# A segment-recurrent attention kernel with a channel MLP: all engines' orders in a block written down whole, each scaled probability write as two operations

## The chip, the cores and the metric

The kernel runs on one core of a Trainium2 chip. The metric is the device time of one launch in microseconds (us). A core has five engines with queues of their own: TensorE (PE in the profile; its weight loads are PEld), VectorE (DVE), ScalarE (ACT), GpSimd (POOL) and SyncE (SP), which issues DMAs.

## What is computed

A layer norm of x (2048 x 512) goes through attention that runs over 64 segments of 32 rows. Each segment sees 8 memory rows ahead of its own, and the attention's first 8 output rows are the memory of the next segment, so segments follow one another. Behind it stands a channel MLP on all rows.

```python
for s in range(n_seg):                       # 64 segments
    xs = x[:, s*32:(s+1)*32, :]
    h = concatenate([mem, xs], axis=1)       # 8 + 32 rows
    q, k, v = h @ Wq, h @ Wk, h @ Wv         # 32 heads of 128
    p = softmax(where(mask, q @ k.T * scale, -1e9))
    o = einsum('bhte,hed->btd', p @ v, Wo)
    mem = o[:, :8, :]
    outs.append(o[:, 8:, :])
h = x + concatenate(outs, axis=1)
y = layernorm(layernorm(h))
h2 = h + gelu(y @ w1 + b1) @ w2 + b2
```

## The kernel before

**How the work is staged.** All weights of the attention lie in SBUF. A block is 4 segments (128 rows of x); s mod 4 is called a segment's *kind* here. A segment has these parts, each a list of recorded operations: `Q0`, `Q1`, `K0`, `K1`, `V0`, `V1` (a projection's two halves, four units each; a unit is four matmuls of 512 columns in tiles of 128 rows x 32 columns, side by side in the array), `SC0` and `SC1` (scores of the memory's queries for half of the heads), `PV0` and `PV1` (their probabilities times values), `PVA` (the same for the 24 other rows, of the segment before), `WO` (eight units of sixteen instructions: output projection), `SA` (scores of the other rows), and `F0`, `F1`, eight units of work that isn't on the segment's own path: in kinds 0, 1, 2 the K, Q, V projections of the next block's last rows, in kind 3 the output projection `wo_B` of the block before. Blocks 0 and 15 have none or few of them. PV0, PV1 and PVA are in tiles of 64 x 128, all other parts named here in tiles of 128 x 32.

**The path through a segment.** Q0 to K1 are copied out of PSUM by ScalarE (`kq0` to `kq3`), transposed by VectorE (`QT`, `KA`), and the memory's queries are laid into `ZC` (`ZCm0`, `ZCm1`, GpSimd). SC0 goes to `sc_softmax`: a maximum on VectorE (`nmc`), two exponentials with their sums on ScalarE (`EC`), then on VectorE for each of the two column sets a reciprocal (`ra`, `rsc`) and a scaled probability write (`PCa`, `PC`), and a transpose (`PTC0`), for which PV0 waits. SC1, PTC1 and PV1 go the same way. PV0's and PV1's results are copied to `OT` (`OTm0`, `OTm1`), WO reads them, VectorE transposes WO's result (`TT`) and adds its halves into `hT` (`hTm`): the memory rows, for which the next segment's Q0 waits. SA's softmax runs beside this path (`nma`, `SA`, `sma`, `rsa`, `PA`, `PTA`) and ends in four GpSimd copies (`BD`), which PVA reads a segment later.

**What sets the order.** Every operation is recorded with what it reads and writes. TensorE's order is written by hand in `ORDERS`: for each kind a list of (part, first unit, end). For the other engines `Sched.schedule` places operations in time: `PLAN` gives an operation's time from its segment's start by kind of operation and of segment, for priority alone; `HOME` names the engine of some that can run on two; else the scheduler takes the free place and the engine that end earliest. Operations that aren't on the path are held behind others by `after=`: the layer norm of a coming block (`ln1`) behind the memory rows, `PA` behind the memory rows, `ZCb` (`qb_fill`) behind KA0, the residual rows (`opA`) and the end of a block's statistics (`nat`) behind PTC1, GpSimd's fold of `wo_B`'s result (`fold`) behind the probability writes. `wire` turns orders into semaphore waits. `align` puts spare weight loads into TensorE's stream so that each segment starts at a given place (`PHASE`) of a block of 256 fetched instructions.

The write whose form is changed, in `sc_softmax` (`even` is 128 x 2, ones in one column for even groups of 32 rows and in the other for odd ones):

```python
S.op("dve", lambda e, sl=sl, xc=xc: e.scalar_tensor_tensor(PC[:, r, :, :, sl], xc, rsc[:, r, sl:sl + 1], ev, ALU.mult, ALU.mult),
     reads=[ek, rk, "even"], writes=[pk], dur=0.305)
```

Of the kernel before, what the change touches and what calls it, by code (L numbers as in the profile page):

```python
# [40 lines left out]
ORDER = ORDERS[0]  # L41
BANK = dict(K0=7, K1=6, Q0=6, Q1=5, V0=7, V1=5, F0=4, F1=6, FB=4, SA=5, WO=7, SC0=3, SC1=2)
PLAN = {"kq2": (1.72,) * 4,
        "QT0": (2.37,) * 4,
        "ZCm0": (2.85,) * 4,
        "kq0": (2.23,) * 4,
        "KA0": (2.87,) * 4,
        "SP0": (-5.14, -4.54, -4.55, -4.02),
        "nmc0": (3.86,) * 4,
        "Ea0": (4.18,) * 4,  # L50
        "EC0": (4.59,) * 4,
        "ra0": (4.66,) * 4,
        "PCa0": (4.86,) * 4,
        "rsc0": (5.1,) * 4,
        "PC0": (5.4,) * 4,
# [1 line left out]
        "VS0": (4.88,) * 4,
        "kq3": (2.79,) * 4,
        "QT1": (3.48,) * 4,
        "ZCm1": (3.97,) * 4,  # L60
        "kq1": (3.65,) * 4,
        "KA1": (4.29,) * 4,
        "SP1": (-1.16, -1.01, -1.18, -1.31),
        "nmc1": (5.19,) * 4,
        "Ea1": (5.51,) * 4,
        "EC1": (5.92,) * 4,
        "ra1": (5.98,) * 4,
        "PCa1": (6.1,) * 4,
        "rsc1": (6.35,) * 4,
        "PC1": (6.55,) * 4,  # L70
        "PTC1": (7.13,) * 4,
        "VS1": (5.61, 5.61, 6.51, 6.21),
        "VSl1": (6.65, 6.5, 6.56, 6.5),
        "OTm0": (6.05, 6.05, 6.05, 6.2),
        "OTm1": (6.85, 7.84, 7.9, 6.64),
        "OTB": (9.67, 11.69, 9.8, 10.06),
        "SAp": (7.58, 6.98, 8.18, 7.88),
        "nma": (10.17,) * 4,
        "SAs": (10.6,) * 4,
        "SAe": (11.07,) * 4,  # L80
        "sma": (11.54,) * 4,
        "rsa": (12.0,) * 4,
        "PA": (12.24,) * 4,
        "PTA": (13.52,) * 4,
        "BD": (15.41,) * 4,
        "OTx0": (7.73, 7.73, 8.22, 7.73),
        "OTx1": (8.9, 8.39, 8.15, 8.0),
        "TT": (9.37,) * 4,
        "hTm": (9.86,) * 4,
        "opA": (17.5, 10.96, 18.73, 17.5),  # L90
        "ZCb": (5.92, 3.35, 3.35, 3.35),
        "kq4": (10.48, 10.48, None, None),
        "KB0": (11.12, None, None, None),
        "QTB0": (None, 28.73, None, None),
        "VSB0": (None, None, 10.48, None),
        "kq5": (9.46, 8.04, None, None),
        "KB1": (12.13, None, None, None),
        "QTB1": (None, 8.75, None, None),
        "VSB1": (None, None, 10.85, None),
        "TTB": (None, None, None, 10.96)}  # L100
# [1594 lines left out]
```

## Time and profile before

| | us |
|---|---|
| three runs | 804.49, 805.81, 806.96 (median 805.81) |
| the profiled execution, first to last instruction | 804.0 |
| TensorE busy / weight loads | 772.7 / 419.3 |
| VectorE busy | 616.6 |
| ScalarE busy | 543.0 |
| GpSimd busy | 350.7 |

The profiled execution's own time is the span of its instructions, 804.0; nothing else of it was recorded, and the runs' times are whole launches. A group's line in the profile has source line, engine, operation, out<-in by the program's names, shapes, count, then busy us and the mean length in ns, then idle time ahead of it and what ended it. A timeline's line has start, length, engine, source line, operation and count; like instructions that follow one another are merged.

### The profile page before, as it was taken

The numbers are of one execution on the slowest core, as the hardware profiler recorded it, in microseconds if no ns is written. First come the engines' busy times: TensorE is split into PE (matmuls) and PEld (weight loads), VectorE is DVE, ScalarE is ACT, GpSimd is POOL, SyncE is SP. The second block draws the span as 40 slices with busy tenths as digits, with TensorE's granted clock in tenths as the row PEclk, the third lists the DMA queues.
The fourth block names the chain that finished last, engine by engine and source line by source line (L and its number), as shares of the span: only waits on it lengthen the run. The fifth ranks groups of instructions, "written<-read, shape, count | busy, mean of one in ns | idle before, by whom it ended". The sixth has DMA issues, their size and how long they took to land.

```text
span 804.0 us, 43669 instructions
## 1 busy us (share of the span) xinstructions
PE 772.7 (96%) x19317; PEld 419.3 (52%) x18821; DVE 616.6 (77%) x1975; ACT 543.0 (68%) x1618; POOL 350.7 (44%) x886
## 2 busy tenths in 40 slices
...
DMA packets 65450, 48.04 MB, mean 60 GB/s; under 512 B 29028, under 2 KB 61676, under 8 KB 65260
## 3 DMA queue, kind: packets, MB, share of 16 engines
...
q14 instruction: 40, 0.33, 0.1%
q10 hardware_dynamic: 332, 0.27, 0.1%
...
## 4 chain that ended last, share of the span: by engine, by line
PE 91%; DVE 3%; DMA 2%; SPq 2%; ACT 1%; issue 0%
PE ps L873 43%; PE ps L1176 16%; PE ps L606 7%; PE quad L1584 6%; PE ps L1577 5%; PE ps L1215 4%; PE quad L1080 3%; DMA WQ<-in_A_Wq_dram 2%; SPq L776 2%; PE ps L1110 2%; PE quad L1042 2%; PE ps L1370 2%; PE quad L1148 1%; PE quad L1085 1%; DVE PC L1067 1%; ACT kq L891 1%
## 5 line engine op out<-in xcount | busy, mean ns | idle before, releaser
L873 PE MATMUL ps<-WQ,hT 128*32 128x512 bf16 x2048 | 157.0, 382 | 3.5 <-DVE hT L1182 3.3
L1176 PE MATMUL ps<-WO,OT 128*32 128x256 bf16 x4224 | 141.5, 275 | 1.0 <-ACT OT L891 1.0
L873 PE MATMUL ps<-WV,hT 128*32 128x512 bf16 x1780 | 138.1, 379 | 0.0
L892 ACT ACTIVATE kq<-ps 128x512 bf16<-128x512 f32 x146 | 87.2, 597 | 57.5 <-PE ps L873 57.2
L1131 POOL TENSOR_TENSOR PA<-SA,rsa 128x256 bf16<-128x256 f32 x64 | 39.8, 622 | 181.4 <-DVE rsa L1124 169.6
L891 ACT CAST kq<-ps 128x512 bf16<-128x512 f32 x160 | 93.3, 583 | 29.8 <-PE ps L873 29.8
L1176 PEld LDWEIGHTS ps<-WO,OT 128*32 128x32 bf16 x4224 | 96.2, 96 | 23.6 <-ACT OT L891 4.0
L1137 POOL COPY BD<-PTA 32x192 bf16<-32x192 bf16 x256 | 95.7, 374 | 16.5 <-DVE PTA L1133 0.8
L1067 DVE SCALAR_TENSOR_TENSOR PC<-EC,rsc,even 128x128 bf16<-128x128 f32 x256 | 94.5, 370 | 6.7
L873 PE MATMUL ps<-WK,hT 128*32 128x512 bf16 x1292 | 92.3, 379 | 0.0
L873 PEld LDWEIGHTS ps<-WQ,hT 128*32 128x32 bf16 x2048 | 56.4, 96 | 63.7 <-issue 19.3
L914 DVE STREAM_TRANSPOSE KALL<-kq 128x256 f32<-128x256 f32 x160 | 70.5, 441 | 21.3 <-ACT kq L891 19.0
L891 ACT CAST VS<-ps 128x512 bf16<-128x512 f32 x189 | 83.9, 444 | 0.9
L1059 ACT ACTIVATE EC<-quad,nmc 128x64 f32<-128x64 f32 x252 | 76.8, 310 | 5.7
L606 PE MATMUL ps<-WK,hT 128*32 128x512 bf16 x756 | 74.3, 379 | 0.0
L891 ACT CAST OT<-quad 128x128 bf16<-128x128 f32 (+1 forms) x208 | 68.4, 352 | 4.9 <-PE quad L1085 0.7
L914 DVE STREAM_TRANSPOSE QT<-kq 128x256 f32<-128x256 f32 x128 | 57.0, 446 | 16.1 <-ACT kq L892 15.0
L873 PEld LDWEIGHTS ps<-WV,hT 128*32 128x32 bf16 x1780 | 49.4, 96 | 34.9 <-issue 1.0
L1580 ACT ACTIVATE WQ<-ps,b1t 128x512 bf16<-128x512 f32 x42 | 28.9, 687 | 52.0 <-PE ps L1577 52.0
L1122 ACT ACTIVATE SA<-SA 128x256 f32<-128x256 f32 x64 | 26.7, 417 | 52.2 <-DVE SA L1121 48.8
L873 PEld LDWEIGHTS ps<-WK,hT 128*32 128x32 bf16 x1292 | 35.9, 97 | 46.6 <-issue 20.2
L1228 POOL TENSOR_TENSOR opT<-TTB,TTS 32x64 bf16<-32x64 f32 x128 | 40.3, 315 | 31.7 <-DVE opT L1182 22.5
...
## 6 DMA issues: line engine op xcount, KB each, us to landing
...
```

The costliest lines, as they stand in the source:

```text
L606: return e.add_instruction(mybir.InstMatmult(name="I-%d" % (4000000 + _kept[0]), engine=mybir.EngineType.PE, start_tensor_calc=start, stop ...
L873: ins = e.matmul(o, l, m, start=(k == 0), stop=(k == DC - 1), tile_position=(0, 32 * j), skip_group_check=True)
L891: return {"act": (lambda e: e.copy(out, src), t_act(n, ps_)), "dve": (lambda e: e.tensor_copy(out, src), 0.155 + 1.0e-3 * n * fast)}
L892: return {"act": (lambda e: e.mul(out, src, scale_), t_act(n, ps_)), "dve": (lambda e: e.tensor_scalar(out, src, scale_, None, ALU.mult), ...
L914: S.op("dve", lambda e: e.transpose(out, src), reads=[("kq", i)], writes=[key], dur=t_dve(256) + 0.02)
L1059: return e.activation(EC[:, r, sl, :], o[:, sl, :], ACTF.Exp, bias=nmc[:, r, sl:sl + 1], accum_out=smc[:, r, sl:sl + 1])
L1067: S.op("dve", lambda e, sl=sl, xc=xc: e.scalar_tensor_tensor(PC[:, r, :, :, sl], xc, rsc[:, r, sl:sl + 1], ev, ALU.mult, ALU.mult), reads= ...
L1137: S.narrow(S.op("pool", lambda e, j=j, rows=rows: e.tensor_copy(BD[rows, par, :, j, :, :], PTA[rows, :, 0:NA, :]), reads=["PTA"], writes=[ ...
L1176: ins = e.matmul(ps[bank][32 * j:32 * j + 32, 0:256], lhs(slot(h)), wo_cols(h, b), start=(k == 0), stop=(k == 15), tile_position=(0, 32 * ...
L1228: return e.tensor_tensor(o[32 * q:32 * q + 32, c:c + 2], x, y, ALU.add)
L1577: ins = e.matmul(ps[bank][:, 0:SBT], W1[:, cc, fc * P:(fc + 1) * P], hnT_of(k)[:, cc, :], start=(cc == 0), stop=(cc == DC - 1))
L1584: S.op("pe", lambda e: e.matmul(quad[:, t, :], gT_of(k, fc)[:, t * P:(t + 1) * P], W2[:, fc, :], start=(fc == 0), stop=(fc == FC - 1)), re ...
```

## The change

`ORDERS` becomes a list of (part, first unit, end, shift) by kind, `EMIT` names the order in which parts are recorded, and `PLAN`, `HOME` and the new `DUR` give time, engine and length for nearly every operation and kind. The times are now binding: on each engine the planned operations are chained in the order of STEP x segment + time. The `after=` orders named above are gone, and the operations they held are planned too. A second reader of a PSUM bank on the same engine (VectorE, ScalarE) no longer waits for the first (`soft`). TensorE's stream is aligned once a block instead of once a segment. Each probability write becomes two `tensor_scalar`, for even and odd groups of rows, with two scalars a row; each may run on VectorE or GpSimd. Some copies change engine (in kinds 0 and 1 the copy `kq5` and SA's prefill go to ScalarE).

```diff
-        "PTC0": (5.74,) * 4,
+        'PTC0': (5.665, 5.653, 5.691, 5.678),
...
+        ('PC0x', 1): 'pool',
+        ('PC0y', 1): 'dve',
...
-STEP = 10.28
+STEP = 10.008
+PHASE = 160
...
+        rows = {e: [] for e in ENGINES}
+        for o in self.rec:
+            at = planned(o)
+            if at is not None and not o.is_dma:
+                o.eng = HOME.get((o.kind, o.tag[0] % 4), o.eng)
+                if o.alts:
+                    o.fn, o.dur = o.alts[o.eng]
+                o.dur = DUR.get((o.kind, o.eng), o.dur)
+                rows[o.eng].append((STEP * o.tag[0] + at, o.gidx, o))
+        for row in rows.values():
+            row.sort()
+            for a, b in zip(row, row[1:]):
+                b[2].order = a[2]
+                a[2].succ.append(b[2])
...
-                if p.eng == E and E not in self.self_sync:
+                if p.eng == E and (E not in self.self_sync or (p in o.soft and E != "pool")):
                     continue
...
-            if PHASE and o.tag is not None and o.tag[0] != seg:
-                seg = o.tag[0]
-                owed = (LATE.get(seg, PHASE[seg % 4]) - at) % FETCH_N
+            if o.tag is not None and o.tag[0] // 4 > seg:
+                seg = o.tag[0] // 4
+                owed = (PHASE - at) % FETCH_N
...
-                x = EC[:, r, sl, :]
-                xc = bass.AP(x.tensor, x.offset, [list(x.ap[0]), [0, 2], [1, 64]])
-                S.op("dve", lambda e, sl=sl, xc=xc: e.scalar_tensor_tensor(PC[:, r, :, :, sl], xc, rsc[:, r, sl:sl + 1], ev, ALU.mult, ALU.mult),
-                     reads=[ek, rk, "even"], writes=[pk], dur=0.305)
+                for b in range(2):
+                    f = lambda e, sl=sl, b=b: e.tensor_scalar(PC[:, r, b, :, sl], EC[:, r, sl, :], rsc[:, r, sl:sl + 1], even[:, b:b + 1], ALU.mult, ALU.mult)
+                    S.either({"dve": (f, 0.19), "pool": (f, 0.3)}, reads=[ek, rk, "even"], writes=[(pk[0], b, r)], kind="%s%d%s" % (pk[0], r, "xy"[b]))
...
-            after = [S.last_writer.get(("hTm", (s + 1) % RING))] if s + 1 < NS else []
...
-                    qb_fill(s + 1, [S.last_writer[("KA", s % 2, 0)]])
+                    qb_fill(s + 1)
```

What this does to the engines' orders is shown at three places, in a segment of kind 1 in the middle. A row has line, operation, out<-in, size and count.

TensorE before, from the last F unit ahead of PV0 (`WQ,hB`; `quad<-PTC,VS` and `quad<-PTC,VBD` are PV0 or PV1, `quad<-BD,VS` is PVA) to WO's rest:

```order
L873 MATMUL ps<-WQ,hB 32x512 x4
L1080 MATMUL quad<-PTC,VS 128x2x16 x8
L1085 MATMUL quad<-PTC,VBD 128x128 x2
L1148 MATMUL quad<-BD,VS 128x2x24 x16
L873 MATMUL ps<-WQ,hB 32x512 x4
L1176 MATMUL ps<-WO,OT 32x256 x16
L1080 MATMUL quad<-PTC,VS 128x2x16 x8
L1085 MATMUL quad<-PTC,VBD 128x128 x2
L1176 MATMUL ps<-WO,OT 32x256 x48
```

And in the changed kernel (its line numbers are its own):

```order
L1136 MATMUL ps<-WQ,hB 32x512 x4
L1355 MATMUL quad<-PTC,VS 128x2x16 x8
L1360 MATMUL quad<-PTC,VBD 128x128 x2
L1136 MATMUL ps<-WQ,hB 32x512 x4
L1422 MATMUL quad<-BD,VS 128x2x24 x16
L1450 MATMUL ps<-WO,OT 32x256 x16
L1355 MATMUL quad<-PTC,VS 128x2x16 x8
L1360 MATMUL quad<-PTC,VBD 128x128 x2
L1450 MATMUL ps<-WO,OT 32x256 x48
```

One F unit has moved from behind PVA to between PV0 and PVA; the other kinds have it so too.

VectorE before, from SC0's first reciprocal to PTC1:

```order
L1064 RECIPROCAL rsc<-smc 128x1
L1067 SCALAR_TENSOR_TENSOR PC<-EC,rsc,even 128x128
L1064 RECIPROCAL rsc<-smc 128x1
L1050 TENSOR_REDUCE nmc<-quad 128x2
L1067 SCALAR_TENSOR_TENSOR PC<-EC,rsc,even 128x128
L1069 STREAM_TRANSPOSE PTC<-PC 128x128
L1064 RECIPROCAL rsc<-smc 128x1
L1067 SCALAR_TENSOR_TENSOR PC<-EC,rsc,even 128x128
```

And in the changed kernel:

```order
L1340 RECIPROCAL rsc<-smc 128x1
L1342 TENSOR_SCALAR PC<-EC,rsc,even 128x64
L1340 RECIPROCAL rsc<-smc 128x1
L1327 TENSOR_REDUCE nmc<-quad 128x2
L1342 TENSOR_SCALAR PC<-EC,rsc,even 128x64
L1344 STREAM_TRANSPOSE PTC<-PC 128x128
L1340 RECIPROCAL rsc<-smc 128x1 x2
L1342 TENSOR_SCALAR PC<-EC,rsc,even 128x64 x2
L1344 STREAM_TRANSPOSE PTC<-PC 128x128
```

A whole write has become a half here; the other halves of this kind are on GpSimd. In the other kinds three halves stand ahead of PTC0 on VectorE and one on GpSimd.

GpSimd before, from one segment's PA to the fold that follows its BD copies:

```order
L1131 TENSOR_TENSOR PA<-SA,rsa 128x4x2x32
L928 COPY ZC<-QT 128x8x2x8
L935 COPY ZC<-QTB 128x16x2x8
L928 COPY ZC<-QT 128x8x2x8
L1137 COPY BD<-PTA 32x4x48 x4
L1228 TENSOR_TENSOR opT<-TTB,TTS 32x8x8 x4
```

And in the changed kernel, from kind 0's PA to kind 1's:

```order
L1405 TENSOR_TENSOR PA<-SA,rsa 128x4x2x32
L1504 TENSOR_TENSOR opT<-TTB,TTS 32x8x8
L1411 COPY BD<-PTA 32x4x48 x2
L1205 COPY ZC<-QT 128x8x2x8
L1411 COPY BD<-PTA 32x4x48
L1342 TENSOR_SCALAR PC<-EC,rsc,even 128x64 x2
L1411 COPY BD<-PTA 32x4x48
L1342 TENSOR_SCALAR PC<-EC,rsc,even 128x64 x2
L1405 TENSOR_TENSOR PA<-SA,rsa 128x4x2x32
```

The BD copies are spread, and two pairs of probability writes stand among them.

More of the change, by code (lines that the diff above doesn't have):

```diff
@@ L24 @@
 FETCH_AT, PADS, SLIP = 65, 8, 24
-PHASE = (0, 64, 128, 192)
-LATE = {60: 60}
 KEEP = True
@@ L29 @@
 PAUSES, PAUSE_IN, PAUSE_US = 3, 64, 0.5
-HALVES = ("kq", "KA", "QT", "ZCm", "VS", "VSl", "nmc", "Ea", "EC", "ra", "rsc", "PCa", "PC", "PTC", "OTm", "OTx", "KB", "QTB", "VSB")
+HALVES = ("kq", "KA", "QT", "ZCm", "VS", "VSl", "nmc", "Ea", "EC", "ra", "rsc", "PCa", "PC", "PTC", "OTm", "OTx", "KB", "QTB", "VSB", "opB")
 BONUS = {}
@@ L41 @@
[L41 to L55, printed above, removed]
-        "PTC0": (5.74,) * 4,
[L57 to L100, printed above, removed]
@@ L163, in op @@
                 deps.add(w)
+                if not (excl and w in self.lookers.get(k, ())):
+                    hard.add(w)
             if excl:
@@ L169, in op @@
                 deps.add(w)
+                hard.add(w)
             deps.update(self.readers.get(k, ()))
+            hard.update(self.readers.get(k, ()))
         deps.update(a for a in after if a is not None)
         deps.discard(o)
+        o.soft = deps - hard
+        for k in o.reads:
+            self.lookers.setdefault(k, set()).add(o)
+        for k in o.writes:
+            self.lookers[k] = set()
         o.deps = sorted(deps, key=lambda d: d.gidx)
@@ L252, in schedule @@
             topo.append(o)
-            for d in o.deps + ([o.prev] if o.prev is not None else []):
+            for d in o.deps + [p for p in (o.prev, o.order) if p is not None]:
                 left[d] -= 1
@@ L299, in schedule @@
             for d in o.deps:
-                t = max(t, d.start + d.dur + self.lat(d, o))
+                t = max(t, d.start + (0.0 if d.eng == o.eng and d in o.soft else d.dur + self.lat(d, o)))
+            if o.order is not None:
+                t = max(t, o.order.start + o.order.dur - OVERLAP[o.eng])
             if o.eng in ("sp", "act") and o.prev is not None:
@@ L578, with directions @@
 MC, MR, MF, MH = 1, 2, 3, 4
[L581 removed]
+def directions(order):
     back, last = {}, None
[L584 to L589 removed]
+    for n, lo, hi, was in order:
+        pack = ("A", was) if n in ("K0", "K1", "Q0", "Q1", "V0", "V1") else "B" if n[0] == "F" else None
+        for u in range(lo, hi if pack else lo):
+            if u == 0:
+                back[n] = last == (pack, DC - 1)
+            last = pack, DC - 1 - u % DC if back.get(n, False) != (u >= DC) else u % DC
         if pack is None:
             last = None
[L592 to L596 removed]
     return back
@@ L920, in k_seg, with k_split @@
             par, a0 = s % 2, (s % 2) * HP + 8 * r
-            kq_T(r, bank, words(KALL[:, a0:a0 + 8]), ("KA", par, r))
+            kq_T(r, bank, words(KALL[:, a0:a0 + 8]), ("KA", par, r), more=[("KA", par, 2)] * r)
+        def k_split(s, back):
+            par = s % 2
+            lhs, reads, slot_ = pack_a(s)
+            for n, bank in enumerate((BANK["K1"], BANK["K1b"])):
+                part = (256 * n, 256 * n + 256)
+                passes(lhs, reads, [(WK, "WK", 1, bank, cols_kq)], back != (n == 1), slot_, part)
+                i, key = (1, 6)[n], ("KA", par, 1 + n)
+                a0 = par * HP + 8 + 4 * n
+                dst = kq[:, 1, 4 * n:4 * n + 4]
+                S.either(copy2(dst, ps[bank][:, part[0]:part[1]].rearrange("p (a b e) -> p a e b", a=4, b=2), 256), reads=[("ps", bank)], writes=[("kq", i)])
+                src = dst.rearrange("p a e b -> p a (e b)").bitcast(F32)
+                S.op("dve", lambda e, o=words(KALL[:, a0:a0 + 4]), src=src: e.transpose(o, src), reads=[("kq", i)], writes=[key], dur=t_dve(128))
         def q_seg(s, r, bank):
```

547 lines of the change are left out of this document (404 added, 143 removed), and 9 rows, old and new, of tables (EMIT, ORDERS).

## The prediction

> **What bounds the kernel now.** I read the page's busy times first, then its chain of work that ended last, then one stretch of the middle.
>
> ```profile
> PE 772.7 (96%) x19317; PEld 419.3 (52%) x18821; DVE 616.6 (77%) x1975; ACT 543.0 (68%) x1618; POOL 350.7 (44%) x886
> PE 91%; DVE 3%; DMA 2%; SPq 2%; ACT 1%; issue 0%
> 300.00:400.00 100.00, 99.98 (x2872) 56.00 (x2732) 90.24 (x296) 77.07 (x241) 50.29 (x130) 1.00 0.10 25
> ```
>
> TensorE holds 91% of the chain, and in the middle it is never out of work by this count. But a matmul counts as busy until its modelled end, so a short hole behind it is covered. Holes are read from the starts. In the next rows (TensorE's timeline, the tail of a segment of kind 0, then the tail of the kind 1 behind it) the columns are start, length, line, operation and count; four matmuls of 512 columns, one to each column quarter of the array, are one unit.
>
> ```profile
> 335.06 0.39 PE L873 MATMUL ps<-WK,hB 128*32 128x512 bf16 x4
> 335.41 0.27 PE L1080 MATMUL quad<-PTC,VS 64*128 64x32 bf16 x8
> ...
> 338.25 0.39 PE L873 MATMUL ps<-WK,hB 128*32 128x512 bf16 x4
> ...
> 339.42 0.40 PE L873 MATMUL ps<-WQ,hT 128*32 128x512 bf16 x4
> ...
> 343.43 0.83 PE L873 MATMUL ps<-WV,hT 128*32 128x512 bf16 x12
> 344.07 0.40 PE L873 MATMUL ps<-WQ,hB 128*32 128x512 bf16 x4
> ...
> 345.27 0.40 PE L873 MATMUL ps<-WQ,hB 128*32 128x512 bf16 x4
> 345.65 0.27 PE L1080 MATMUL quad<-PTC,VS 64*128 64x32 bf16 x8
> ...
> 345.82 0.36 PE L1148 MATMUL quad<-BD,VS 64*128 64x48 bf16 x16
> 346.11 0.40 PE L873 MATMUL ps<-WQ,hB 128*32 128x512 bf16 x4
> 346.35 0.62 PE L1176 MATMUL ps<-WO,OT 128*32 128x256 bf16 x16
> 346.91 0.27 PE L1080 MATMUL quad<-PTC,VS 64*128 64x32 bf16 x8
> ...
> 347.17 1.49 PE L1176 MATMUL ps<-WO,OT 128*32 128x256 bf16 x48
> 348.49 0.42 PE L1110 MATMUL ps<-KALL,QT 128*32 128x32 bf16 x32
> 348.74 1.06 PE L873 MATMUL ps<-WQ,hB 128*32 128x512 bf16 x16
> 349.75 0.40 PE L873 MATMUL ps<-WQ,hT 128*32 128x512 bf16 x4
> ```
>
> A unit followed by its like takes 0.22 or less (343.43 to 344.07: 0.64 for three). Three holes stand out: ahead of PV0 (335.06 to 335.41, 345.27 to 345.65: 0.35 and 0.38), ahead of PV1 (346.35 to 346.91: 0.56 for four groups), ahead of Q0 (348.49 to 349.75). How much of them is waiting? The next rows tell: the kernel's last PVA, and one PV1 whose PTC was early.
>
> ```profile
> 702.90 1.64 POOL L1137 COPY BD<-PTA 32x192 bf16<-32x192 bf16 x4 [0.82 <-DVE PTA L1133]
> 704.41 1.04 PE L1370 MATMUL ps<-xr,QTB 128*128 128x512 bf16 x4
> 705.38 0.37 PE L1148 MATMUL quad<-BD,VS 64*128 64x48 bf16 x16
> 705.69 1.04 PE L1370 MATMUL ps<-xr,QTB 128*128 128x512 bf16 x4
> 192.29 0.61 PE L1176 MATMUL ps<-WO,OT 128*32 128x256 bf16 x16
> 192.44 0.31 DVE L1069 STREAM_TRANSPOSE PTC<-PC 128x128 f32<-128x128 f32 x1
> 192.83 0.27 PE L1080 MATMUL quad<-PTC,VS 64*128 64x32 bf16 x8
> ```
>
> PVA at 705.38 had its last input at 704.54, and still comes 0.97 behind four matmuls that need 4 x 0.22: **0.1 is lost with nothing to wait for**, where the tile changes from one that spans the rows (128*128, 128*32) to the halves (64*128). At 192.83, PTC had ended at 192.75, 0.08 ahead rather than the 0.06 of other segments (345.59 to 345.65 below), and PV1 came 0.54 behind its WO piece, hardly less than 0.56. So about 0.1 ahead of PV0 and of PV1 is the change of tile. Waiting is what is left: 0.02 (kind 0) to 0.05 (kind 1) at PV0, 0.01 at PV1. Leaving the halves costs as much: behind PV1's last two matmuls, and from PVA to the next unit, 0.29 in both places (345.82 to 346.11) for what streams in less than 0.2.
>
> [...]
>
> Ahead of Q0, the chain from WO's end over TT and hTm is 1.17 (338.25 to 339.42), and the work put there, SA and four F units, 0.25 + 4 x 0.22 = 1.13: 0.03 is waited, in kind 1 0.12.
>
> **The change part by part.** *TensorE's order.* From SC0 to PV0 there are still eleven units and SC1, between WO and Q0 still SA and four F units, in every kind. One thing differs in all kinds: one F unit goes from behind PVA to between PV0 and PVA. Before, PV0 and PVA stand together in the halves' tile; PV0's start to WO's start is 345.65 to 346.35, 0.70. After: PV0 to F like PV1 to WO, 346.91 to 347.17, 0.26; F to PVA like F to PV0 less its waiting, 0.35 - 0.03 = 0.32; PVA to WO like PVA to F, 0.29. Sum 0.87, **0.17 more**: the tile changes six times in a segment instead of four. It is in the 56 segments 4 to 59 and in 63: 57 x 0.17 = **+9.7 us**. Nothing hides it, as TensorE is the bound. Lower bound 0 (first rival), upper 0.2 each (two changes of 0.1), 11.4. PVA's readers on ScalarE come later by as much; the next segment's WO needs them, so nobody is late.
>
> *Probability writes.* Vector rows of the same segment, and the groups that price the halves (between the bars stand busy us and mean ns):
>
> ```profile
> 344.09 0.12 DVE L1064 RECIPROCAL rsc<-smc 128x1 f32<-128x1 f32 x1
> 344.25 0.38 DVE L1067 SCALAR_TENSOR_TENSOR PC<-EC,rsc,even 128x128 bf16<-128x128 f32 x1
> ...
> 344.68 0.29 DVE L1050 TENSOR_REDUCE nmc<-quad 128x2 f32<-128x128 f32 x1
> 344.89 0.36 DVE L1067 SCALAR_TENSOR_TENSOR PC<-EC,rsc,even 128x128 bf16<-128x128 f32 x1
> 345.28 0.31 DVE L1069 STREAM_TRANSPOSE PTC<-PC 128x128 f32<-128x128 f32 x1
> ...
> 346.54 0.31 DVE L1069 STREAM_TRANSPOSE PTC<-PC 128x128 f32<-128x128 f32 x1
> L1064 DVE RECIPROCAL rsc<-smc 128x1 f32<-128x1 f32 x192 | 26.4, 137 | 0.0
> L1182 DVE TENSOR_TENSOR opT<-TT 64x96 bf16<-64x96 f32 x100 | 26.4, 264 | 2.3
> L1182 DVE TENSOR_TENSOR hT<-TT 64x32 bf16<-64x32 f32 x98 | 19.6, 200 | 2.4
> L809 POOL TENSOR_SCALAR rst<-agg 128x1 f32<-128x1 f32 x12 | 3.1, 258 | 4.1 <-DVE agg L808 3.1
> L935 POOL COPY ZC<-QTB 128x256 bf16<-128x256 bf16 x49 | 19.5, 397 | 9.1 <-DVE KALL L914 9.1
> ```
>
> No row shows half a write (64 elements, two row scalars). On VectorE it lies between 137 ns (one element) and 264 (two tensors of 96 elements); I take 200, the 32-element row. On GpSimd it lies between 258 and 397; I take 330. Kinds 0, 2 and 3 put six halves on VectorE and two on GpSimd, kind 1 four and four. PTC0's path, from 344.09: reciprocal, half (0.20 for 0.38), reciprocal, half, nmc (it needs SC1), half, transpose: 0.38 + 0.36 become three times 0.20, so PTC0 is done some 0.12 sooner. TensorE can use only the waiting, 0.03 x 57 = **-1.7**. PTC1 is sooner by 0.25, worth 0.01 x 57 = **-0.5**, as WO and PV1 now stand 0.17 later anyway. At 264 a half, PTC0 would be 3 x 0.264 - 0.74 = 0.05 later than now, and PV0 with it: the upper end, +2.9; at 137 TensorE still has only the 0.03 to gain.
>
> [...] No run here shows a half yet.
>
> The new wait is PTC0 on GpSimd; behind it on VectorE stand the second half's reciprocal and writes. In kind 1 two halves go through GpSimd one behind the other, from the first reciprocal's end (0.12) to 0.12 + 2 x 0.38 = 0.88, where today's last write ends at 345.25, 1.16: inside, if GpSimd is free, and a BD copy (0.41 each: 1.64 for four) stands ahead of them. The price if not: 0.1 in 14 segments, 1.4.
>
> *Moved copies and dropped orders.* In kind 1 Q0 waits 0.12, since its hTm pair lasts longer beside a running GpSimd copy:
>
> ```profile
> 349.20 0.48 DVE L1182 TENSOR_TENSOR hT<-TT 64x32 bf16<-64x32 f32 x2
> 349.04 0.39 POOL L1230 COPY TTS<-TTB 64x256 f32<-64x256 f32 x1
> ```
>
> (0.48 against two of 0.20.) The fold that does it is in kind 0's tail afterwards, so the 0.09 may only move: between 0 and 14 x 0.12 = 1.7, I take **-1.0**. A copy to kq goes from VectorE to ScalarE, SA's prefill is shared out; ScalarE is at 77%, off the path. [...] The waits dropped between two reads of one bank sit on copies that aren't late: 0.
>
> *Segments without F* (1 to 3, 60 to 62) wait longer at PV0:
>
> ```profile
> 58.10 0.27 PE L1080 MATMUL quad<-PTC,VS 64*128 64x32 bf16 x8 [0.38 <-DVE rsc L1064]
> ```
>
> There the chain counts in full: 0.12 at PV0 and 0.1 at PV1, times 6, **-1.3**. The opening and the channel MLP are unchanged.
>
> Sum: 9.7 - 1.7 - 0.5 - 1.0 - 1.3 = **+5.2 us**. The profiled execution's span is 804.0, so 809.2; the three runs' median is 805.81, 1.8 above that span, and carried to it the time is **811.0**.
>
> **The rivals.** *Faster: the holes are waits.* If the 0.1 ahead of PV0 and PV1 were waiting for PTC, and the F unit went between PV0 and PVA free, the earlier PTC0 (0.12) and PTC1 (0.1 of its 0.25) would come off in full: 57 x 0.22 = 12.5, with the other gains 2.3 about 791. It decides as soon as an F unit followed by PVA takes under 0.25. For it: the waits' view does put these holes down to VectorE. Against it: 705.38, 192.83. Chance 0.17, with smaller gains of other origin counted in.
>
> *No difference: every wait goes.* The tile changes cost 9.7, but all waiting vanishes: 1.7 and 0.5, Q0's 0.03 and 0.12 in the mean 0.065 x 57 = 3.7, and the six openings' 0.38 x 6 = 2.3: 8.2 back, +1.5, 807.3. For it: VectorE, 90% busy, gets free time. Against: the 1.17 chain is unchanged. Chance 0.17.
>
> *Slower still.* GpSimd holds PTC0 in kind 1 (1.4), the crowd on VectorE ahead of TT in kind 2 (prefills, a statistic) makes hTm late by 0.1 (1.4), and halves of 0.264 instead of 0.20 take back PV0's 1.7 and add 2.9: each alone or all, 7.4 more, up to 818.4. Chance 0.16.
>
> **How the numbers follow.** Forecast 811.0 (809 to 813) with 0.50. The range leaves out the first rival alone: 802 to 819. A 0.3% step (2.4 us) is about what a measurement can tell from no change. Slower by more: 0.50 + 0.16 = 0.66; within: 0.17; faster: 0.17.
>
> **What would show it.** In the changed kernel's TensorE timeline PV0's start to WO's start should be 0.87; F to PVA 0.32 with BD long done; PV0 behind its unit by 0.32 to 0.33; Q0 still 1.17 behind WO's end; the halves 0.20 and 0.33. An F unit between PV0 and PVA that costs 0.22, or a PV1 less than 0.5 behind its WO piece, would make the prediction wrong.

## The result, and the profile after

| | before | after |
|---|---|---|
| runs side by side, us | 804.49 to 807.17, median 806.38 (4) | 838.01, 835.74, 839.55, 836.46: median 837.24 |
| profiled execution, first to last instruction | 804.0 | 836.3 |
| VectorE busy / GpSimd busy | 616.6 / 350.7 | 633.9 / 374.5 |

The changed kernel is slower: 1.0395 times the time before (95% interval 1.037 to 1.042). The direction was forecast; +31 us instead of +5 was not.

The changed kernel's page (busy times, the chain that ended last) and the window from 300 to 400 us (length, then each engine's busy time, TensorE's clock, DMA share, GB/s):

```profile
PE 793.0 (95%) x19317; PEld 414.2 (50%) x18632; DVE 633.9 (76%) x2178; ACT 535.4 (64%) x1602; POOL 374.5 (45%) x955
PE 48%; DVE 39%; ACT 4%; POOL 3%; DMA 3%; issue 2%; SPq 2%; DVEq 0%; POOLq 0%
300.00:400.00 100.00, 98.09 (x2680) 52.12 (x2566) 88.02 (x310) 70.74 (x220) 52.70 (x137) 1.00 0.10 26
```

The chain says it at once: TensorE alone was 91% of it, now VectorE holds 39%. The window hardly shows it (98 instead of 100 of 100 us), since a matmul counts as busy until its modelled end (379 ns in the median, while units start 0.22 us apart). So again the holes are read from starts. TensorE's timeline of the changed kernel, a segment of kind 0 from K1 to the next segment's first projection, then PV0 of the kind 1 behind it:

```profile
346.56 0.83 PE L1136 MATMUL ps<-WK,hT 128*32 128x512 bf16 x12
347.51 0.31 PE L1319 MATMUL quad<-KALL,ZC 128*32 128x64 bf16 x16
...
349.94 0.39 PE L1136 MATMUL ps<-WK,hB 128*32 128x512 bf16 x4
350.40 0.27 PE L1355 MATMUL quad<-PTC,VS 64*128 64x32 bf16 x8
...
350.66 0.40 PE L1136 MATMUL ps<-WK,hB 128*32 128x512 bf16 x4
350.99 0.37 PE L1422 MATMUL quad<-BD,VS 64*128 64x48 bf16 x16
351.30 0.62 PE L1450 MATMUL ps<-WO,OT 128*32 128x256 bf16 x16
351.85 0.27 PE L1355 MATMUL quad<-PTC,VS 64*128 64x32 bf16 x8
...
353.43 0.39 PE L1136 MATMUL ps<-WK,hB 128*32 128x512 bf16 x4
...
354.94 0.40 PE L1136 MATMUL ps<-WK,hT 128*32 128x512 bf16 x4 [0.20 <-DVE hT L1456]
...
360.81 0.38 PE L1136 MATMUL ps<-WQ,hB 128*32 128x512 bf16 x4
361.46 0.27 PE L1355 MATMUL quad<-PTC,VS 64*128 64x32 bf16 x8 [0.27 <-DVE rsc L1340]
```

Four things differ from before. SC0 stands 0.95 behind the last three units of K1, which need 0.65 (346.56 to 347.51). PV0 stands 0.46 behind its unit in kind 0 and 0.65 in kind 1 (it was 0.35 and 0.38). PV0's start to WO's start is 0.90 (350.40 to 351.30; it was 0.70). And the next segment's first projection comes 1.51 behind WO's end (353.43 to 354.94), not 1.17.

Over all segments of blocks 1 to 14, the differences of such starts, as means by kind and added up over the four kinds, give the time of a block (in this table, and wherever values by kind are given below, a unit's time is the start of its last matmul, some 0.02 behind its first):

| us a block | before | after | difference |
|---|---|---|---|
| WO's end to the unit ahead of PV0 | 28.34 | 28.90 | +0.56 |
| that unit to PV0 | 1.36 | 2.01 | +0.65 |
| PV0 to WO | 2.79 | 3.58 | +0.79 |
| WO to PV1 | 2.25 | 2.22 | -0.03 |
| PV1 to WO's end | 6.39 | 6.33 | -0.07 |
| block | 41.13 | 43.03 | +1.91 |

Fourteen blocks make 26.7 of the 32.3 us between the profiled executions, segments 1 to 3 and 60 to 63 make 3.9, and the opening, up to PV0 of segment 1, makes 1.7. The opening varies between runs: it took 58.1 us before and 59.8 in the changed kernel, but 58.8 in the probe kernel below, which differs from the changed one only at its end, and 56.8 to 59.9 in all traces. So single runs are compared by their blocks below.

Why PV0 is late is in VectorE's and GpSimd's timelines of that kind 1, the groups of the page, and a line of the waits' view (who waits for what: us in all, times, longest):

```profile
359.61 0.12 DVE L1340 RECIPROCAL rsc<-smc 128x1 f32<-128x1 f32 x1
359.77 0.33 DVE L1342 TENSOR_SCALAR PC<-EC,rsc,even 128x64 bf16<-128x64 f32 x1
360.15 0.84 POOL L1342 TENSOR_SCALAR PC<-EC,rsc,even 128x64 bf16<-128x64 f32 x2 [0.20 <-DVE rsc L1340]
360.39 0.32 DVE L1342 TENSOR_SCALAR PC<-EC,rsc,even 128x64 bf16<-128x64 f32 x1
361.09 0.31 DVE L1344 STREAM_TRANSPOSE PTC<-PC 128x128 f32<-128x128 f32 x1 [0.38 <-POOL PC L1342]
L1342 DVE TENSOR_SCALAR PC<-EC,rsc,even 128x64 bf16<-128x64 f32 x349 | 106.9, 328 | 6.3
L1342 POOL TENSOR_SCALAR PC<-EC,rsc,even 128x64 bf16<-128x64 f32 x163 | 70.2, 439 | 29.2 <-DVE rsc L1340 20.3
DVE PTC L1344 <- POOL PC L1342: 14.0, 37, 0.4
```

A half takes 328 ns on VectorE and 439 on GpSimd, where 200 and 330 were forecast. It is hardly shorter than the whole write was (0.36 to 0.38). In kind 1 the two halves on GpSimd end at 360.99, and VectorE, done at 360.71, waits for them with the transpose. They start at 360.15, 0.54 behind the first reciprocal's start: a BD copy holds GpSimd until 359.95, and what the other 0.20 waits for isn't settled by the trace. In the other kinds the third half on VectorE ends last. Counted from SC0's start (medians by kind), PTC0 starts at 2.38 to 2.41 before, at 2.49 to 2.52 in kinds 0, 2 and 3 of the changed kernel, and at 2.69 in kind 1.

The other two holes have one cause in common. VectorE's and GpSimd's timelines ahead of SC0, and at the end of the segment:

```profile
346.09 0.73 POOL L1499 TENSOR_TENSOR TTB<-TTB,TTS 64x256 f32<-64x256 f32 x1
346.17 0.97 DVE L1405 TENSOR_TENSOR PA<-SA,rsa 128x256 bf16<-128x256 f32 x1
347.03 0.43 DVE L1177 STREAM_TRANSPOSE KALL<-kq 128x256 f32<-128x256 f32 x1
353.90 0.72 POOL L1499 TENSOR_TENSOR TTB<-TTB,TTS 64x256 f32<-64x256 f32 x1
354.14 0.74 DVE L1456 TENSOR_TENSOR hT<-TT 64x32 bf16<-64x32 f32 x2
```

The product PA (of the segment of kind 3 before; it runs in kind 0's time) has come from GpSimd to VectorE. It lasts 0.97 beside GpSimd's fold add (0.42 where nothing of the kind runs beside it), and KALL, for which SC0 waits, stands behind it on VectorE. The hT pair lasts 0.74 beside the second fold add, 0.39 otherwise.

### The profile page after: what moved, and what is told of

It is laid out like the page before. It is cut to its first block, busy times and chain, and to the rows that moved or that the text cites. A ratio compares the mean times of both kernels' runs of the same rounds, so it can differ in the third digit from the quotient of the medians.

```text
span 836.3 us, 43954 instructions
## 1 busy us (share of the span) xinstructions
PE 793.0 (95%) x19317; PEld 414.2 (50%) x18632; DVE 633.9 (76%) x2178; ACT 535.4 (64%) x1602; POOL 374.5 (45%) x955
## 4 chain that ended last, share of the span: by engine, by line
PE 48%; DVE 39%; ACT 4%; POOL 3%; DMA 3%; issue 2%; SPq 2%; DVEq 0%; POOLq 0%
PE ps L1450 15%; PE ps L1136 11%; PE quad L1833 6%; DVE PC L1342 5%; DVE KALL L1177 4%; PE ps L1826 4%; PE quad L1355 3%; DVE QT L1177 3%; DVE TT L1462 3%; DVE hT L1456 3%; DVE PTC L1344 2%; DMA WQ<-in_A_Wq_dram 2%; POOL PC L1342 2%; PE quad L1422 2%; DVE nma L1395 2%
## 5 line engine op out<-in xcount | busy, mean ns | idle before, releaser
L1136 PE MATMUL ps<-WQ,hT 128*32 128x512 bf16 x1668 | 127.6, 382 | 1.5 <-DVE hT L1456 1.5
L1136 PE MATMUL ps<-WK,hT 128*32 128x512 bf16 x1604 | 123.0, 380 | 3.4 <-DVE hT L1456 3.3
L1155 ACT ACTIVATE kq<-ps 128x512 bf16<-128x512 f32 x160 | 96.2, 601 | 33.4 <-PE ps L1136 31.7
L1342 DVE TENSOR_SCALAR PC<-EC,rsc,even 128x64 bf16<-128x64 f32 x349 | 106.9, 328 | 6.3
L1154 ACT CAST OT<-quad 128x384 bf16<-128x384 f32 (+1 forms) x223 | 78.1, 359 | 39.0 <-PE quad L1360 36.9
L1342 POOL TENSOR_SCALAR PC<-EC,rsc,even 128x64 bf16<-128x64 f32 x163 | 70.2, 439 | 29.2 <-DVE rsc L1340 20.3
L1397 ACT ACTIVATE SA<-SA 128x256 f32<-128x256 f32 x64 | 26.7, 417 | 80.7 <-DVE SA L1396 80.3
L1136 PEld LDWEIGHTS ps<-WQ,hT 128*32 128x32 bf16 x1668 | 44.5, 97 | 56.8 <-issue 14.9
L1205 POOL COPY ZC<-QT 128x128 bf16<-128x128 bf16 x64 | 18.6, 290 | 105.6 <-DVE QT L1177 104.2
L1405 POOL TENSOR_TENSOR PA<-SA,rsa 128x256 bf16<-128x256 f32 x32 | 20.4, 638 | 92.4 <-ACT kq L1155 81.7
L1462 DVE STREAM_TRANSPOSE TT<-ps 128x256 f32<-128x256 f32 x66 | 29.7, 450 | 42.2 <-PE ps L1450 41.1
## 6 DMA issues: line engine op xcount, KB each, us to landing
WV<-in_A_Wv_dram SPq DMA_DIRECT2D x4, 1024.0 KB, 10.3
```

The costliest lines, as they stand in the source:

```text
L1136: ins = e.matmul(o, l, m, start=(k == 0), stop=(k == DC - 1), tile_position=(0, 32 * j), skip_group_check=True)
L1154: return {"act": (lambda e: e.copy(out, src), t_act(n, ps_)), "dve": (lambda e: e.tensor_copy(out, src), 0.155 + 1.0e-3 * n * fast)}
L1155: return {"act": (lambda e: e.mul(out, src, scale_), t_act(n, ps_)), "dve": (lambda e: e.tensor_scalar(out, src, scale_, None, ALU.mult), ...
L1342: f = lambda e, sl=sl, b=b: e.tensor_scalar(PC[:, r, b, :, sl], EC[:, r, sl, :], rsc[:, r, sl:sl + 1], even[:, b:b + 1], ALU.mult, ALU.mult)
L1462: S.op("dve", lambda e: e.transpose(tt.rearrange("p c q t -> p (c q t)"), ps[bank][:, 0:256]), reads=[("ps", bank)], writes=[("TT", par)], ...
```

## The experiments

Each kernel is the changed one with an edit, or the one before with a part of the change. Times stand beside runs of the kernel before on the same chip, medians 805.0 to 806.5. Where a kernel has one run, the verdict rests on the stretches of its trace.

### The F unit back behind PVA (f_behind_pva)

```diff
-... ('PV0', 0, 1, 0), ('F1', 3, 4, 0), ('PVA', 0, 1, 0), ...
+... ('PV0', 0, 1, 0), ('PVA', 0, 1, 0), ('F1', 3, 4, 0), ...
```

> The changed kernel with its one F unit moved back from between PV0 and PVA to behind PVA; nothing else. Theory (two changes of tile more): in the changed kernel PV0's start to WO's start is 0.892 where an F unit lies between, 0.69 where none does; so 0.20 x 57 = 11.4 comes off, 826 (824 to 828), PV0's start to WO's start 0.69 again and PV0's own hole unchanged (0.65 in kind 1, 0.43 to 0.47 in the others). Rival (the F unit is free there, the time is lost elsewhere): 835 to 839.

837.75 us: **nothing came off**. PV0 to WO was 0.69 again in kinds 1 and 2, as the theory had it, but the 0.20 turned up right behind. TensorE's and VectorE's timelines in kind 1, then GpSimd's and TensorE's in kind 0:

```profile
405.33 0.62 PE L1450 MATMUL ps<-WO,OT 128*32 128x256 bf16 x16
405.72 0.31 DVE L1344 STREAM_TRANSPOSE PTC<-PC 128x128 f32<-128x128 f32 x1 [0.42 <-POOL PC L1342]
406.08 0.27 PE L1355 MATMUL quad<-PTC,VS 64*128 64x32 bf16 x8
...
393.09 0.74 POOL L1411 COPY BD<-PTA 32x192 bf16<-32x192 bf16 x2
393.56 0.27 PE L1355 MATMUL quad<-PTC,VS 64*128 64x32 bf16 x8
...
393.98 0.37 PE L1422 MATMUL quad<-BD,VS 64*128 64x48 bf16 x16
```

In kind 1, PV1 now stands 0.75 behind WO's start (0.55 with the unit in between), since its transpose waits for GpSimd's halves. In kinds 0 and 3, PV0 to PVA is 0.42 instead of 0.17: PVA comes there 0.15 behind the last of the BD copies, which ends at 393.83 in the kind 0 shown and stands on GpSimd behind a half. The unit and its two changes of tile lay beside waits that the halves had made. The theory was wrong as a price in this kernel, the rival's price right. What the unit costs where nothing is late had to be tried on the other kernel (below).

### One write again instead of two halves (one_write)

```diff
-                for b in range(2):
-                    f = lambda e, sl=sl, b=b: e.tensor_scalar(PC[:, r, b, :, sl], EC[:, r, sl, :], rsc[:, r, sl:sl + 1], even[:, b:b + 1], ALU.mult, ALU.mult)
...
+                S.op("dve", lambda e, sl=sl, xc=xc: e.scalar_tensor_tensor(PC[:, r, :, :, sl], xc, rsc[:, r, sl:sl + 1], ev, ALU.mult, ALU.mult),
+                     reads=[ek, rk, "even"], writes=[pk], dur=0.305)
```

> The changed kernel with one scalar_tensor_tensor on VectorE for each scaled write again, in place of the two halves on VectorE and GpSimd; engines' orders else as they are. Theory (PTC0 is late because a half takes 0.33 on VectorE and 0.44 on GpSimd): PV0's hole falls from 0.65, 0.47, 0.46, 0.43 to 0.34 to 0.36 in every kind, some 0.66 a block or 9.3, and 2 to 3 more in the six segments without F: 825 (823 to 828). Rival (PTC0 is late because of what the new order puts ahead of it on VectorE, whatever the write): the holes stay over 0.42 and the time over 833.

821.1 us: 16 us off, more than expected. PV0's hole fell to 0.34, 0.34, 0.38 and 0.37 (kinds 0 to 3). Of the 17.2 us between the profiled executions, 10.8 came off blocks 1 to 14: 8.2 of it at PV0, and most of the rest at the hT pair, since without halves GpSimd reaches the second fold add at another time and the next segment's first projection came 1.26 behind kind 0's WO, not 1.41 (means). Another 3.4 came off segments 1 to 3 and 60 to 63. The other 3.0 are this run's opening of 56.8 us, the shortest of all; two_undone below, with the same writes, has 58.6. So the halves cost some 14 us, not quite half of the loss.

### Kind 0's two places (kind0_aside)

```diff
-        'PA': (12.298, 12.417, 13.166, 12.48),
+        'PA': (12.298, 12.417, 13.166, 12.95),
...
-        'f1b': (None, None, None, 18.953),
+        'f1b': (None, None, None, 20.25),
...
```

> The changed kernel with two places of the order changed in kind 0: VectorE's product PA comes behind the transpose to KALL, not ahead of it, and GpSimd's second fold add comes in the next segment, not beside the hT pair. Theory (operand traffic of GpSimd's add slows VectorE's adds, and what stands ahead of KALL holds SC0): kind 0's Q0 comes 1.17 behind WO's end, not 1.51, and SC0 comes 0.21 behind K1's last unit, not 0.49: (0.34 + 0.28) x 14 = 8.7 off, 828.5 (827 to 831). Rival (ScalarE's copies hold both): 835 to 839, with hT still 0.7 long or KALL still as late.

841.15 us, slower (blocks 1 to 14 took 605.6 us, 602.5 in the changed kernel): neither the theory's time nor the rival's. PA took 0.42 again and SC0 came on time, but PA and what follows it (PTA, a statistic) then stood ahead of the next transposes, and SC1 came 0.33 late instead. And the number in the plan is a place in an order, not a time: the fold add ran as soon as GpSimd was free, on the second hT operation rather than on the first (VectorE's and GpSimd's timelines behind kind 0):

```profile
355.40 0.89 DVE L1456 TENSOR_TENSOR hT<-TT 64x32 bf16<-64x32 f32 x2
355.52 0.72 POOL L1499 TENSOR_TENSOR TTB<-TTB,TTS 64x256 f32<-64x256 f32 x1
```

The pair grew to 0.89 from 0.39, which speaks for the collision; that operand traffic is its cause no run shows, only the lengths. The edit itself made no better order.

### All three at once (three_undone)

> All three edits at once: F behind PVA, one write per probability block, kind 0's two places changed. What is left of the change is the written-out order with its moved copies. Theory (the three terms add): 837.2 - 11.4 - 12 - 8.7 = 805 (803 to 809), no more than 0.4% from the kernel before. Rival (a hole that is closed opens again behind it): 812 or more.

816.81 us, 1.0137 times the time before (1.0117 to 1.0156). The terms don't add: kind 0's edit makes things worse by itself, and the time is in the rival's range (812 or more). But here PV0 to WO was 0.69 to 0.71 with WO to PV1 at 0.56 to 0.58: with the halves gone the 0.20 of the F unit comes off and stays off.

### The F unit alone, on the kernel before (before_f_between)

```diff
-... ('PV0', 0, 99), ('PVA', 0, 99), ('F1', 3, 4), ...
+... ('PV0', 0, 99), ('F1', 3, 4), ('PVA', 0, 99), ...
```

> The kernel before with one part of the change alone: its F unit goes from behind PVA to between PV0 and PVA. Theory (two tile changes, nothing else late): PV0's start to WO's start goes from 0.70 to 0.89, PV0's and PV1's holes stay at 0.34 and 0.56: 806 + 0.20 x 57 = 817 (815 to 819). Rival (the 0.2 is taken from waits, as the changed kernel lost nothing when the unit was moved back): 805 to 809, with a wait that was there gone.

817.42 us against 806.54: **+10.9**. TensorE's timeline in kind 0, PV0 and WO:

```profile
381.81 0.27 PE L1080 MATMUL quad<-PTC,VS 64*128 64x32 bf16 x8
...
382.70 0.62 PE L1176 MATMUL ps<-WO,OT 128*32 128x256 bf16 x16
```

0.89 instead of 0.70, in all kinds, with PV0's and PV1's holes as they were (0.34 and 0.55). The unit between PV0 and PVA, with the two changes of tile that it adds, costs 0.20 a segment when nobody else is late. (By blocks it makes 0.76 of the 0.83 added; PV1 to WO's end also grew, by 0.12 in kinds 0 and 1, and most of that came off other waits.)

### The halves alone, on the kernel before (before_halves)

The same `tensor_scalar` pair in place of each write, all on VectorE, at the write's place.

> The kernel before with the other part alone: two tensor_scalar halves in place of each probability write, all on VectorE, in the place of the one. Theory (two halves take 0.63 from start to end where the one write takes 0.38, two such writes ahead of PTC0 and two more ahead of PTC1): PV0's hole 0.34 becomes 0.75 to 0.85, and PV1 comes later too: 57 x 0.45 to 57 x 0.95, 832 to 860. The price on record (0.20 a half): 804 to 809.

853.96 us: **+47**, within the theory's range. VectorE's and TensorE's timelines in kind 0:

```profile
399.46 0.69 DVE L1066 TENSOR_SCALAR PC<-EC,rsc,even 128x64 bf16<-128x64 f32 x2
400.49 0.40 PE L873 MATMUL ps<-WK,hB 128*32 128x512 bf16 x4
...
401.26 0.27 PE L1079 MATMUL quad<-PTC,VS 64*128 64x32 bf16 x8 [0.37 <-DVE rsc L1064]
...
402.88 0.27 PE L1079 MATMUL quad<-PTC,VS 64*128 64x32 bf16 x8 [0.31 <-DVE PTC L1068]
```

Two halves last 0.69 where the write lasted 0.38; PV0's hole is 0.77, and PV1 is late too (0.92 behind WO's start in the mean of kind 0, 0.56 before). With two of eight halves on GpSimd, and four in kind 1, the changed kernel loses some 14 us to the halves rather than 47.

### What makes a half dear (probe)

Eleven operations, six of each, were added to the changed kernel behind the last projection, each waiting for the one before:

```diff
+        probe(0, "dve", lambda e: e.tensor_scalar(PC[:, 0, 0, :, 0], x1, r1, e1, ALU.mult, ALU.mult))
...
+        probe(3, "dve", lambda e: e.tensor_scalar(PC[:, 0, 0, :, 0], x1, 0.5, None, ALU.mult))
```

> The changed kernel with single operations added on idle engines behind the last projection, six of each, each behind the one before: the half as it is, with its output side by side, with one row scalar, with a constant instead, the old write of 128, the half of one element, a plain copy, both halves in one tensor_scalar, and on GpSimd the half, with output side by side, and a copy. Theory A (a fixed price for an operation of this kind on these operands): 0.30 to 0.33 for all of 64 elements, 0.26 for one element. Theory B (the second row scalar): 0.33 with two, 0.2 to 0.25 with one or none. Theory C (the output at every second place): 0.33, and 0.2 to 0.25 with output side by side. On GpSimd 0.41 to 0.44 for the half with nothing beside it, if it isn't VectorE that makes it dear.

The trace's durations by source line (least, median and greatest of six in ns): the half; its output side by side; one row scalar; a constant; the old write; the half of one element; on GpSimd the half and a copy:

```profile
L1851 DVE TENSOR_SCALAR PC<-EC,rsc,even x6: 308/326/764, 729.6 to 739.9; 128x64 bf16<-128x64 f32 x6
L1852 DVE TENSOR_SCALAR PC<-EC,rsc,even x6: 314/314/316, 740.3 to 742.0; 128x64 bf16<-128x64 f32 x6
L1853 DVE TENSOR_SCALAR PC<-EC,rsc x6: 223/347/775, 743.2 to 748.4; 128x64 bf16<-128x64 f32 x6
L1854 DVE TENSOR_SCALAR PC<-EC x6: 205/294/358, 748.8 to 750.5; 128x64 bf16<-128x64 f32 x6
L1855 DVE SCALAR_TENSOR_TENSOR PC<-EC,rsc,even x6: 310/364/365, 750.7 to 756.2; 128x128 bf16<-128x128 f32 x6
L1856 DVE TENSOR_SCALAR PC<-EC,rsc,even x6: 268/272/276, 756.5 to 762.5; 128x1 bf16<-128x1 f32 x6
L1859 POOL TENSOR_SCALAR PC<-EC,rsc,even x6: 412/416/554, 774.0 to 776.7; 128x64 bf16<-128x64 f32 x6
L1861 POOL CAST PC<-EC x6: 236/237/237, 780.3 to 781.8; 128x64 bf16<-128x64 f32 x6
```

GpSimd's last folds ran beside some of them, beside all six with one row scalar, so the least is read. One element with two row scalars costs 268, 64 elements 308; with one row scalar 223, with none 205. Both halves in one `tensor_scalar` of 128 took 359 to 366. Theory C falls (314 with output side by side), and a part of A and of B holds: nearly all of a half is a fixed price (268 of 308), and the second row scalar is some 85 ns of it. On GpSimd 412 of the 439 were there with nothing beside it.

### The second row scalar left out (one_scalar)

```diff
-                    f = lambda e, sl=sl, b=b: e.tensor_scalar(PC[:, r, b, :, sl], EC[:, r, sl, :], rsc[:, r, sl:sl + 1], even[:, b:b + 1], ALU.mult, ALU.mult)
+                    f = lambda e, sl=sl, b=b: e.tensor_scalar(PC[:, r, b, :, sl], EC[:, r, sl, :], rsc[:, r, sl:sl + 1], None, ALU.mult)
```

> The changed kernel with the halves' second row scalar left out (each half is the exponential times rsc alone; the mask by even isn't applied). Theory (it is the second row scalar that makes a half 0.33; alone a half with one took 0.22): halves of 0.22 to 0.23 on VectorE, shorter ones on GpSimd too, PV0's hole 0.34 to 0.36 in kinds 0, 2 and 3 and under 0.5 in kind 1: 837 less 11 to 15, 822 to 827. Rival (two operations instead of one, whatever each takes): the holes stay over 0.42, 832 or more.

844.2 us, slower still (blocks 1 to 14 took 607.6 us against 602.5): the theory missed. The rival's figures came true, but not as a test of it, since the halves changed their lengths. The groups of its page's view by form:

```profile
L1342 DVE TENSOR_SCALAR PC<-EC,rsc 128x64 bf16<-128x64 f32 x349 | 91.1, 283 | 6.2
L1342 POOL TENSOR_SCALAR PC<-EC,rsc 128x64 bf16<-128x64 f32 x163 | 80.5, 508 | 28.2 <-DVE rsc L1340 23.8 <-ACT VS L1154 3.4 <-ACT EC L1334 0.6
```

On VectorE the halves became shorter (283 for 328), on GpSimd longer (508 for 439), and PTC0 and PTC1 wait for whichever ends last: PV0's hole was 0.43, 0.70, 0.51 and 0.53. GpSimd's half ended last in every kind, 0.11 to 0.35 behind VectorE's last (medians), so GpSimd's halves hold the path as much as VectorE's. Those on VectorE took 0.26 beside a GpSimd half and 0.36 beside a BD copy (medians), not the 0.22 expected. Those on GpSimd took 0.46 with nothing of VectorE's beside them, so VectorE explains only a part of their length; why one with a single row scalar is longer than one with two there was not tried.

### Kind 1's half on VectorE (kind1_vector)

```diff
-        'PCa0y': (5.079, 5.023, 4.903, 4.887),
+        'PCa0y': (5.079, 4.887, 4.903, 4.887),
...
-        ('PCa0y', 1): 'pool',
+        ('PCa0y', 1): 'dve',
```

> The changed kernel with one half of kind 1 (the second of PTC0's first pair) on VectorE, as in the other kinds, not on GpSimd. Theory (in kind 1 two halves one behind the other on GpSimd, 0.42 and 0.46, end 0.1 before PTC0): PV0's hole in kind 1 falls from 0.65 to 0.45 to 0.48, 2.5 off, 833 to 836. Rival (GpSimd isn't what ends last there): the hole stays over 0.6.

835.85 us, within the changed kernel's own runs (835.74 to 839.55); blocks 1 to 14 took 602.2 us against 602.5. The time lies in the theory's range, but the gain doesn't: the hole in kind 1 fell only to 0.57, between theory and rival, and WO to PV1 grew there from 0.55 to 0.60. VectorE's and GpSimd's timelines:

```profile
402.22 0.51 POOL L1342 TENSOR_SCALAR PC<-EC,rsc,even 128x64 bf16<-128x64 f32 x1 [0.54 <-DVE rsc L1340]
402.77 0.31 DVE L1344 STREAM_TRANSPOSE PTC<-PC 128x128 f32<-128x128 f32 x1 [0.22 <-POOL PC L1342]
```

One half less on GpSimd, but the reciprocal for the other comes later behind VectorE's two, and the transpose still waits for GpSimd. Two halves in a row there were a part of kind 1's hole, not all.

### What is left: the order itself (two_undone, rest_tidied, fold_aside)

First the write and the F unit undone, and nothing else:

> One write per block again and F behind PVA, everything else as changed: what is left of the change is its written-out order with its moved copies. Theory (the F unit costs 0.20 a segment as soon as the halves no longer hold PV1 and PVA): one_write's 821.1 less 0.19 x 57 = 10.8, 810.3 (808 to 812), and the rest over the kernel before, some 4, stands ahead of SC0 in kinds 0 and 2 (7.33 and 7.24 from WO's end to the unit ahead of PV0, against 7.04 to 7.14). Rival (F stays free): 819 or more.

812.47 us, 1.0077 times the time before (1.0055 to 1.0098), just above the range. A block is 41.47 us (42.26 with one_write, 41.13 before): the F unit gives 0.79 a block as soon as the halves are gone. What remains is 6.5 us, 4.8 of it in blocks 1 to 14. The greater part stands where expected, from WO's end to the unit ahead of PV0 in kinds 0 and 2 (7.32 and 7.24; 7.08 and 7.13 before). Another 0.09 a block stands at PV0 in kinds 2 and 3: there the first probability write lasts 0.45 to 0.50 beside a BD copy on GpSimd that starts within 0.06 of it.

Then a wider mending of the order (F behind PVA and one write, PA on GpSimd and OTB's copy on ScalarE in kind 0 again, the second fold add ahead of the layer norm step, kind 1's opT pair behind SA):

> F behind PVA and one write, as in three_undone, but the other edits made anew: in kind 0 the product PA is back on GpSimd and the copy to OTB back on ScalarE, GpSimd's second fold add comes ahead of the layer norm step and so ahead of the hT pair; in kind 1 VectorE's opT pair comes behind the SA steps again. Theory (VectorE's adds and GpSimd's add hold each other up; what stands ahead of the transposes to QT and KALL holds SC0 and SC1): kind 1's Q0 1.17 behind WO's end, the way from WO's end to the unit ahead of PV0 7.04 to 7.06 in all kinds (7.37, 7.30, 7.24, 7.04 in three_undone): 0.32 + 0.26 + 0.2 a block, 11 us, 806 (803 to 809). Rival (a wait takes another's place): 812 to 817.

813.62 us (1.0095, 1.0076 to 1.0115): the rival. Kind 0's way fell from 7.37 to 7.08, kind 1's from 7.30 to 7.09, but kind 2's rose to 7.37, and kind 0's PV0 hole to 0.44, as the fold's copy had come beside a probability write (VectorE's and GpSimd's timelines):

```profile
379.46 0.59 DVE L1302 SCALAR_TENSOR_TENSOR PC<-EC,rsc,even 128x128 bf16<-128x128 f32 x1
379.50 0.39 POOL L1460 COPY TTS<-TTB 32x256 f32<-32x256 f32 x1
```

0.59 for a write that takes 0.36 to 0.38 otherwise. Last, two_undone with kind 0's fold alone put aside:

```diff
+        ('OTB', 3): 'act',
+        ('PA', 3): 'pool',
...
+        'f0b': (None, None, None, 12.9),
+        'f0c': (None, None, None, 12.95),
+        'f03': (None, None, None, 16.6),
```

> two_undone with kind 0 alone changed: the copy to OTB back on ScalarE, the product PA back on GpSimd and ahead of the fold add there, so that the add (0.72) runs beside VectorE's transposes instead of beside PA, and the fold's copy and first sum out of the way of the probability writes. Theory (in two_undone VectorE holds SC0 of kind 0 because PA takes 0.96 beside GpSimd's add, 0.42 without): kind 0's way from WO's end to the unit ahead of PV0 falls from 7.33 to 7.05 to 7.10 with PV0's hole still 0.34 and PVA on time: 14 x 0.25 = 3.5 off, 809 (807.5 to 810.5). Rival (a wait takes its place, as in rest_tidied, where PV0's hole grew by 0.11 and PVA's place by 0.13): 811 to 814.

810.69 us beside 805.01 on its chip; its ratio, 1.0077 (1.0053 to 1.0101), is that of two_undone, so by time nothing is told apart, and it lies between theory and rival. By the trace kind 0 did what the theory said (7.08 for 7.32, PV0's hole 0.35, PVA on time), and the add stood beside transposes without making them longer (GpSimd's and VectorE's timelines):

```profile
375.78 0.61 POOL L1365 TENSOR_TENSOR PA<-SA,rsa 128x256 bf16<-128x256 f32 x1
376.47 0.73 POOL L1459 TENSOR_TENSOR TTB<-TTB,TTS 64x256 f32<-64x256 f32 x1
376.35 0.45 DVE L1134 STREAM_TRANSPOSE KALL<-kq 128x256 f32<-128x256 f32 x1 [0.41 <-ACT kq L1111]
...
383.34 0.53 DVE L1416 TENSOR_TENSOR hT<-TT 64x32 bf16<-64x32 f32 x2
```

But GpSimd's work behind it moved, and the second add met the hT pair (0.53): kind 1's way rose from 7.08 to 7.16. A block is 41.35 us, 0.12 less than in two_undone and 0.22 above before; the opening in its trace was 1.2 us longer than two_undone's. No version came out ahead of the kernel before.

## Why the prediction was wrong

In the order in which they were undone, the 31 us are by the runs' times: the halves 16 (837.2 to 821.1), the F unit 9 (to 812.5), the order 6.5 (to 806). Without the openings the traces give 14.2, 10.3 and 6.0.

The direction was right because of the F unit alone: the other terms of the sum stood at zero or below, and but for PTC1's -0.5 (WO to PV1 lost 0.03 a block) each came out above.

- **The F unit, +9.7.** The mechanism was right and the size nearly: 0.20 instead of 0.17 a segment, +10.9 when it is the only change. The reservation that was missing: a unit costs nothing where the next part waits anyway. Moved back in the changed kernel it gave 0, as PTC1 (kinds 1 and 2) and BD (kinds 0 and 3) were late by as much; with the halves gone they weren't. The first rival, that holes are waits and the unit is free, was wrong for the kernel before.
- **Probability writes, -1.7, -0.5 and -1.3: the step that failed.** "On VectorE it lies between 137 ns (one element) and 264 (two tensors of 96 elements); I take 200". The rows that made the bounds have no row scalars; the half has two and took 328, outside of the bounds, and GpSimd's 439 lay outside of 258 to 397. Instead of 0.12 sooner, PTC0 came some 0.12 later in kinds 0, 2 and 3, and 0.28 later in kind 1; instead of -3.5 us the halves cost some 14. The upper end that the prediction gave was +2.9 at PV0. (Three times 0.20 for 0.38 + 0.36 is 0.14 sooner, not 0.12; only 0.03 of it counted.) GpSimd's pair in kind 1, put at 0.12 to 0.88 behind the first reciprocal's start, ran from 0.54 to 1.38. The third rival had the right places (GpSimd holds PTC0 in kind 1, longer halves), but priced from the same rows it ended at 818.
- **Q0 behind kind 1, -1.0, "may only move".** It moved, and grew: the collision went to the tail of kind 0 and cost 0.34 in most segments there (0.22 more than before in the mean), while kind 1's tail gave back 0.10. Together that is some +1.6 us, not -1.0. The row of before had a GpSimd copy beside the pair; now it is an add.
- **Moved copies and dropped orders, 0.** "Off the path" was read from ScalarE's share and from each operation's slack, not from what it would stand ahead of. In kind 0, OTB's copy and PA now stand on VectorE ahead of KALL, for which SC0 waits. The order costs some 6 us. That kind 0's 0.23 a block comes from PA ahead of KALL and beside the fold add is shown by kind0_aside, where SC0 came on time with PA behind KALL, and by fold_aside, where it did with PA and the copy moved away. For kind 2's 0.10 only the trace speaks (ScalarE's copy to kq starts late, behind OTB's), and so it does for the 0.09 at PV0 in kinds 2 and 3; rest_tidied, which moved other work in kind 2, made its way longer. The rest stays open: the dropped bank waits and the alignment once a block are in each of these versions and were not tried alone.
- **Rows named as tests.** PV0 to WO 0.87 was 0.90, F to PVA 0.32 was 0.33, PV1 0.5 or more behind WO was 0.55: as forecast. PV0 behind its unit 0.32 to 0.33 was 0.45 to 0.65 (from the unit's first matmul), Q0's 1.17 was 1.51 behind kind 0, and the halves' 0.20 and 0.33 were 0.33 and 0.44: these failed, and with them the time.
